# Softmax weights times values: full-width products of head pairs, or one head in each half of PE's columns

## The chip, the cores and the metric

One Trainium2 chip, one of its cores. The metric is the device time of one execution in microseconds. A core has five engines with an instruction queue each: PE (matrix products; its weight loads are listed apart as PEld), DVE and ACT (elementwise work and reductions), POOL, and SP, which here issues most DMAs. Each engine works its queue off in order and waits on semaphores where an operand is not there yet.

## The reference

Block-sparse attention, then a gated feed-forward part (SwiGLU) on the heads put side by side. There are 4 batches, 8 heads, 768 positions, head size 64; blocks are 32 positions, so 24 blocks.

```python
scores = (1 / sqrt(D)) * q @ k.T                      # per batch and head, D = 64
mask = |blk_i - blk_j| <= 1  or  blk_i, blk_j in (0, 23)  or  blk_j in sampled_blocks[blk_i]
attn = softmax(where(mask, scores, -1e9))
x = (attn @ v)                                        # to (4 * 768, 512), heads side by side
g = x @ w_gate                                        # 512 -> 1536
out = (g * sigmoid(g) * (x @ w_val)) @ w_out          # 1536 -> 512
```

A query block from 1 to 22 sees 8 key blocks: its window of three, three sampled ones, and the first and last. Query blocks 0 and 23 see all keys ("full rows").

## The kernel before

**Tiling.** A chunk is half a batch, 384 queries, so there are 8 chunks. A chunk has three query tiles of 128 queries, which are four query blocks each. Per batch, blocks 1 to 12 make the first chunk, and 0, 23 and 13 to 22 the second, whose first tile therefore has two full rows and two sparse blocks. There are 76 sparse blocks in chunks 1 to 7 and 12 in chunk 0.

**Number formats.** Chunk 0 computes in float32 (`first_chunk`, `first_block`, `ffn_first`), while the weights are still being decoded and split. The other chunks use pairs of half-precision numbers: each operand is a high and a low part, and a product is the sum of three (high x high, high x low, low x high). A recorded float32 matmul of the program appears as two in the trace.

**A sparse block** (`block`, L1000). Values of the window are loaded by SP, those of the sampled blocks by an indirect DMA of POOL, into one of three buffers `vring` (the tile `vg`: 256 keys as two times 128 partitions, high and low part, 8 heads of 64). PE makes the scores with 32 queries of four heads in the four 32-column strips of its array (L1041); DVE adds the mask and takes the maximum (L1087), ACT the exponential (L1106), ACT and DVE the high and low weights `pp` (L285, L288). SP transposes them by DMA into `pts` (L1131). Then comes the step that is changed, `product` (L1133): per head pair j, 6 matmuls whose weights are the values of both heads, 128 columns, and whose moving operand is the softmax weights of both heads, 2 x 32 columns. The result has 128 partitions (two heads of 64) and 64 columns, of which the two diagonal quarters are wanted: head 0 with its own 32 columns, head 1 with its own.

**x.** The PSUM tile `pv` is one bank of 512 columns: 4 head pairs x 2 blocks x 64. Two blocks fill it, and then `x_high` copies the wanted quarters to the high part of x (`xt`) on ACT, in two instructions of 64 partitions (L1165), and `x_low` takes the difference on DVE, again two (L1170). The ring of `pv` has two banks. Chunk 0 does the same in float32: `product` at L700 with 8 matmuls, `x_keep` at L716 with two copies. In both, the matmuls of a block are 24 x 128 columns of weights (8 in chunk 0).

**Full rows** (`full_rows`, L795) already put one head in each half of PE's columns, L901 and L902.

**Feed-forward.** For chunks 1 to 7, L1328 is x times w_gate and w_val, 12 matmuls of 384 columns per tile of 128 features, and L1374 is h times w_out, 512 columns. Chunk 0 has L1217 and L1252.

**Order.** Nothing is scheduled at run time. A planner (`Plan`) holds every step as a task with an engine, a time in us, its needs, a rank and the buffers it takes; `plan.order()` runs through them and emits the instructions in the order in which its engines took them. Attention ranks ahead of feed-forward work, so PE's feed-forward matmuls fill in where attention waits. A changed time in the table moves tasks on all engines.

Of the kernel before, what the change touches and what calls it, by code (L numbers as in the profile page):

```python
# [13 lines left out]
ALU = mybir.AluOpType  # L14
AX = mybir.AxisListType

P = 128
B, H, S, D = 4, 8, 768, 64
BLK = 32
# [132 lines left out]
def tile_block_sparse_attn_swiglu(  # L152
# [10 lines left out]
    nc = tc.nc  # L163
# [376 lines left out]
    xts = [Buf("xt") for _ in range(NCH)]  # L540
# [17 lines left out]
    def first_chunk(rank):  # L558
# [16 lines left out]
        for t in range(6):  # L575
# [14 lines left out]
            a = add("PE", 1.6, turn, [k0_loads[t // 2], t_id], rank - 2.0, take=[kp])  # L590
            kept.append(add("DVE" if t % 2 else "ACT", 0.7, keep, [a], rank - 2.0, use=[kp]))

        for sub in range(NSUB):
            qbs = ORDER[0][sub * 4 : sub * 4 + 4]
            regbuf, regs = Buf("pregs"), []
            r0 = rank + 0.3 * sub

            def offsets(qbs=qbs, regs=regs):
                _, r = nc.values_load_multi_w_load_instructions(
                    koff[0:1, qbs[0] : qbs[-1] + 1, :].rearrange("p q j -> p (q j)"),  # L600
                    engines=(mybir.EngineType.Pool,),
                    min_val=0,
                    max_val=S - BLK,
                    skip_runtime_bounds_check_because="sampled_blocks holds block numbers",
                )
                regs.extend(r)

            loaded = add("POOL", 0.8, offsets, [t_tab], r0, take=[regbuf])
            for n, qb in enumerate(qbs):
                if n % 2 == 0:  # L610
                    pv = Buf("pv")
                first_block(qb, sub, n, r0 + 0.05 * n, kT, qs[sub], q_there[sub], kept, regs, regbuf, loaded, pv)

    def first_block(qb, sub, n, rank, kT, q, q_there, kept, regs, regbuf, loaded, pv):
# [4 lines left out]
        vf = vring[slot].rearrange("p c l h d -> p c (l h d)").bitcast(F32)  # L619
        qk, e, dg, pt, pts = Buf("qk"), Buf("e"), Buf("pp"), Buf("ffn"), Buf("pts")  # L620
# [77 lines left out]
            nc.scalar.copy(get(pts, f"pts_0_{qb}").bitcast(F32), pt.tile)  # L698

        def product():  # L700
            if n % 2 == 0:
                get(pv, f"pv_0_{qb}")
            pq = pts.tile.bitcast(F32).rearrange("p (g c u q) -> p g c u q", g=2, c=2, u=4)
            pvv = pv.tile.rearrange("p (j b q) -> p j b q", j=4, b=2)

            for j in range(4):
                g, u = divmod(2 * j, 4)
                for cc in range(2):
                    nc.tensor.matmul(
                        pvv[:, j, n % 2], vf[:, cc, 2 * j * D : (2 * j + 2) * D], pq[:, g, cc, u : u + 2, :],  # L710
                        start=cc == 0, stop=cc == 1,
                    )

        cols = slice(sub * P + (n - 1) * BLK, sub * P + (n + 1) * BLK)

        def x_keep():  # L716
            pvv = pv.tile.rearrange("p (j b q) -> p j b q", j=4, b=2)
            for hh in range(2):
                hs_ = slice(hh * D, (hh + 1) * D)
                nc.scalar.copy(  # L720
                    x_f32()[hs_, :, cols].rearrange("p j (b q) -> p j b q", b=2), pvv[hs_, :, :, hh * BLK : (hh + 1) * BLK]
                )
# [12 lines left out]
        a = in_turn("pv", "PE", 2.4, product, [a, vl, vi], rank, take=[] if n % 2 else [pv], use=[pts] + ([pv] if n % 2 else []))  # L735
# [218 lines left out]
    def attention(ci, rank, qtiles):  # L954
        b, half = divmod(ci, 2)
        bt = batches[b]
        for sub in range(NSUB):
# [35 lines left out]
            pv = None  # L993
            for n, qb in enumerate(sparse):
                r = r0 + 0.05 * n
                if n % 2 == 0:
                    pv = Buf("pv")
                block(ci, b, bt, o, sub, n, qb, qbs.index(qb) * BLK, r, tsc, pv)

    def block(ci, b, bt, o, sub, n, qb, col, rank, tsc, pv):  # L1000
        nq = f"{b}_{qb}"
        slot = sparse_no[0] % RING
        direct = ci == 1
# [127 lines left out]
            nc.sync.dma_start_transpose(get(pts, f"pts_{nq}").rearrange("p (m q) -> p m q", q=P), pp.tile)  # L1131

        def product():  # L1133
            if n % 2 == 0:
                get(pv, f"pv_{nq}")
            pq = pts.tile.rearrange("p (g l c u q) -> p g l c u q", g=2, c=2, l=2, u=4)
            pvv = pv.tile.rearrange("p (j b q) -> p j b q", j=4, b=2)

            for j in range(4):
                g, u = divmod(2 * j, 4)  # L1140
                i = 0
                for cc in range(2):
                    for l, m in ((0, 0), (0, 1), (1, 0)):
                        nc.tensor.matmul(  # L1144
                            pvv[:, j, n % 2],
                            vg[:, cc, l, 2 * j : 2 * j + 2, :],
                            pq[:, g, m, cc, u : u + 2, :],
                            start=i == 0,
                            stop=i == 5,
                        )  # L1150
                        i += 1

        cols = slice(sub * P + col - BLK, sub * P + col + BLK)

        def x_views(hh):
            hs_ = slice(hh * D, (hh + 1) * D)
            pvv = pv.tile.rearrange("p (j b q) -> p j b q", j=4, b=2)
            src = pvv[hs_, :, :, hh * BLK : (hh + 1) * BLK]
            xt = xts[ci].tile
            return [src] + [xt[hs_, l, :, cols].rearrange("p j (b q) -> p j b q", b=2) for l in range(2)]  # L1160

        def x_high():
            for hh in range(2):
                src, hi, _ = x_views(hh)
                nc.scalar.copy(hi, src)  # L1165

        def x_low():
            for hh in range(2):
                src, hi, lo = x_views(hh)
                nc.vector.tensor_tensor(lo, src, hi, op=ALU.subtract)  # L1170
# [21 lines left out]
        if n % 2 == 1:  # L1192
# [267 lines left out]
```

## Time and profile before

| | us |
|---|---|
| median of 3 runs | 867.82 |
| the three runs | 865.56, 867.82, 876.54 |
| the profiled execution, its own time | 876.0 |
| the profiled execution, its span from first to last instruction | 874.2 |
| PE busy in that span | 810.1 |

The profile is of one execution. Its page has the busy time of each engine, the chain of work that ended last (followed back from the last instruction to what released each step), and groups of instructions by line. A group reads: line, engine, operation, out<-in by the program's names, count, then busy us and the mean ns of one, then the idle time before them and what ended it. "128*64" at a matmul is rows times columns of the array that it uses; "128x64" its output, partitions times columns. The duration of a matmul is longer than its distance to the next, since they overlap. A timeline row is start, length, engine, line and count of merged instructions, with the length running to the end of the last.

### The profile page before, as it was taken

To read this page: it belongs to the slowest core of one execution; us is meant where nothing else is said; L and a number is where in the kernel's file an instruction comes from. 1 tells how busy PE (TensorE), PEld (TensorE's weight loads), DVE (VectorE), ACT (ScalarE), POOL (GpSimd) and SP (SyncE) were. 2 spreads that over 40 slices of the span, in tenths; PEclk is the share of its full clock that TensorE was granted. 3 is DMA by queue.
4 is the path that set the end of the run, shared out by engine and by line. 5 is a ranking of instruction groups with operands and counts; after the bars stand their busy time and mean duration, and the time that the engine had idled before them with its cause. 6 is when DMAs were issued, how large, how long until landed. Compare 5 with 4: busy or idle time off the path is not lost.

```text
span 874.2 us, 20573 instructions
## 1 busy us (share of the span) xinstructions
PE 810.1 (93%) x7590; PEld 487.9 (56%) x7590; DVE 602.5 (69%) x1924; ACT 522.0 (60%) x1274; POOL 179.6 (21%) x221
## 2 busy tenths in 40 slices
PE   4788899988799988889999999999999899999998
PEld 3577655544465545556556555665556456655653
DVE  4799799875678876777378857884588578841220
ACT  2666474677765775677358666895466567741220
POOL 3141100002032221132123211241124112310220
PEclk9599899999799997999999999999999999999999
DMA  9989966269974997596978794878767864830001
GB/s 228 297 260 278 261 126 211 55 126 216 183 202 121 185 233 146 110 163 148 265 161 151 161 190 84 182 174 235 172 143 137 164 167 80 164 79 25 1 1 36
DMA packets 189972, 138.13 MB, mean 158 GB/s; under 512 B 138480, under 2 KB 150896, under 8 KB 189872
## 3 DMA queue, kind: packets, MB, share of 16 engines
q1 hardware_dynamic: 184240, 119.52, 60.7%
q0 software_dynamic: 5632, 17.31, 8.3%
q8 instruction: 59, 0.97, 0.5%
q14 instruction: 41, 0.34, 0.1%
HBM read 80.68 MB, written 12.58 MB: 107 GB/s over the span
## 4 chain that ended last, share of the span: by engine, by line
PE 66%; DMA 19%; DVE 10%; issue 2%; SPq 2%; ACT 1%; DVEq 0%; ACTq 0%
PE p L1328 33%; PE po L1374 14%; DMA pts<-pp 8%; PE p L1217 5%; PE pv L1144 5%; PE qk L1041 3%; DMA ptsf<-ppf 2%; DMA w2raw<-in_w_dram 2%; DMA qraw<-in_q_dram 2%; DVE w L314 2%; DVE w L315 2%; DMA qs<-qraw 2%; PE po L1252 1%; DMA w<-in_v_dram 1%; DMA kraw<-in_k_dram 1%
## 5 line engine op out<-in xcount | busy, mean ns | idle before, releaser
L1328 PE MATMUL p<-xt,w 128*128 128x384 f16 x2016 | 344.5, 328 | 1.6 <-ACT xt L1165 0.8
L1328 PEld LDWEIGHTS <-w 128*128 128x128 f16 x2016 | 192.7, 99 | 134.8 <-issue 14.9
L1374 PE MATMUL po<-w,h 128*128 128x512 f16 x756 | 170.8, 379 | 0.0
L1028 POOL DMA_INDIRECT vring<-vd,vidx x76 | 72.2, 950 | 336.8 <-PE pv L1144 264.9
L1349 POOL TENSOR_TENSOR h<-act,h 128x384 f16<-128x384 f32 x84 | 82.1, 979 | 274.5 <-ACT h L1346 274.0
L1374 PEld LDWEIGHTS <-h 128*128 128x128 f16 x756 | 71.5, 98 | 83.5 <-issue 4.2
L1144 PEld LDWEIGHTS <-vring 128*128 128x128 f16 x1824 | 64.8, 100 | 36.3 <-issue 27.8
L1144 PE MATMUL pv<-pts,vring 128*128 128x64 f16 x1824 | 67.8, 195 | 18.4 <-DMA pts<-pp 18.3
L1335 DVE SCALAR_TENSOR_TENSOR act<-act,p 128x384 f32<-128x384 f32 x84 | 46.2, 550 | 55.6 <-ACT act L1332 54.6
L1106 ACT ACTIVATE e<-e,nb,es 128x256 f32<-128x256 f32 x132 | 78.2, 593 | 2.2
L1332 ACT ACTIVATE act<-p,gsc 128x384 f32<-128x384 f32 x84 | 48.6, 578 | 47.9 <-PE p L1328 38.8
L1346 ACT CAST h<-act 128x384 f16<-128x384 f32 x84 | 42.5, 505 | 54.4 <-DVE act L1338 53.7
L288 DVE SCALAR_TENSOR_TENSOR pp<-e,rr,pp 128x256 f16<-128x256 f32 x152 | 71.7, 513 | 4.4 <-ACT pp L285 3.5
L285 ACT ACTIVATE pp<-e,rr 128x256 f16<-128x256 f32 x152 | 68.1, 497 | 7.8 <-issue 2.3
L1217 PE MATMUL p<-xt,w 128*128 128x384 f32 x192 | 66.9, 502 | 3.1 <-ACT xt L720 3.1
L1338 DVE SCALAR_TENSOR_TENSOR act<-act,hs,p 128x384 f32<-128x384 f32 x84 | 51.3, 611 | 21.3 <-PE p L1328 18.9
L1087 DVE CUSTOM_DVE_ANT_1 e<-qk,msk 128x256 f32<-128x256 f32 x132 | 50.2, 418 | 13.5 <-PE qk L1041 7.6
L1217 PEld LDWEIGHTS p<-xt,w 128*128 128x128 f32 x192 | 36.2, 194 | 27.7 <-ACT xt L720 3.3
L1165 ACT CAST xt<-pv 64x256 f16<-64x256 f32 x76 | 27.8, 365 | 36.7 <-PE pv L1144 36.1
L1017 DVE COPY kring<-kst 128x256 f16 x228 | 47.1, 262 | 2.5 <-PE qk L1041 2.2
L1170 DVE TENSOR_TENSOR xt<-pv,xt 64x256 f16<-64x256 f32 x76 | 31.9, 420 | 21.1 <-ACT xt L1165 13.8
L1266 ACT ACTIVATE ot<-po,oc 128x512 f32<-128x512 f32 x21 | 14.4, 686 | 47.0 <-PE po L1374 43.1
(183 smaller groups left out, 1082.9 us busy)
## 6 DMA issues: line engine op xcount, KB each, us to landing
vring<-vd SPq DMA_DIRECT2D x76, 192.0 KB
w1raw<-in_w_dram SPq DMA_DIRECT2D x24, 512.0 KB
qs<-qraw SPq DMA_DIRECT2D x84, 128.0 KB
w2raw<-in_w_dram SPq DMA_DIRECT2D x12, 512.0 KB
vfull<-vd SPq DMA_DIRECT2D x12, 512.0 KB
qraw<-in_q_dram SPq DMA_DIRECT2D x42, 128.0 KB
out_dram<-ot SPq DMA_DIRECT2D x20, 256.0 KB
vraw<-in_v_dram SPq DMA_DIRECT2D x9, 512.0 KB
```

The lines of the kernel that those rows point to most:

```text
L285: nc.scalar.activation(hi, src, AF.Copy, scale=scale)
L288: nc.vector.scalar_tensor_tensor(lo, src, scale, hi, op0=ALU.mult, op1=ALU.subtract)
L1028: nc.gpsimd.indirect_dma_start(vf[0:96, 1, :], None, bt.vd, bass.IndirectOffsetOnAxis(ap=vidx[0:96, qb : qb + 1], axis=0))
L1087: nc.vector.tensor_tensor_reduce(ev[:, g], stv[:, g], o.msk[:, n, :].unsqueeze(2).broadcast_to([P, 8, BLK]), scale=1.0, scalar=-3.0e38, op ...
L1106: nc.scalar.activation(ev[:, g], sv[:, g], AF.Exp, bias=nb_[:, g : g + 1], scale=o.es[:, 0:1], accum_out=c["rs"][:, g : g + 1],)
L1144: nc.tensor.matmul(pvv[:, j, n % 2], vg[:, cc, l, 2 * j : 2 * j + 2, :], pq[:, g, m, cc, u : u + 2, :], start=i == 0, stop=i == 5,)
L1217: nc.tensor.matmul(buf.tile[:, 0:T], wst[m][:, f + 1, k_ * P : (k_ + 1) * P], x_f32()[:, k_, :], start=k_ == 0, stop=k_ == NKT - 1,)
L1328: nc.tensor.matmul(t[:, 0:T], w_[:, f, m, k_, :], xt.tile[:, l, k_, :], start=i == 0, stop=i == 11)
L1332: nc.scalar.activation(get(act, f"act_{ci}_{f}"), pg.tile[:, 0:T], AF.Tanh, scale=c["gsc"][:, f : f + 1])
L1338: nc.vector.scalar_tensor_tensor(act.tile, act.tile, c["hs"][:, 1:2], pw.tile[:, 0:T], op0=ALU.mult, op1=ALU.mult)
L1349: nc.gpsimd.tensor_tensor(hv()[:, 1, :], act.tile, hv()[:, 0, :], op=ALU.subtract)
L1374: nc.tensor.matmul(po.tile, hv[:, l, ts_], wo16[:, f, m, :], start=f == 0 and i == 0, stop=f == NF - 1 and i == 2)
```

## The change

Each matmul of the product is split in two, one per head: 64 columns of weights, 32 moving columns, and the output in its own half of the partitions (0 to 63 or 64 to 127). The two heads' matmuls alternate. A block has 48 matmuls and not 24 (16 and not 8 in chunk 0), of a quarter of the size. All that is computed is wanted, so a block needs 4 x 32 columns of the bank and four blocks fill it. x is taken once per query tile, in one instruction of 128 partitions on ACT and one on DVE; a tile with two full rows has two sparse blocks and takes their half of the bank.

```diff
-                if n % 2 == 0:
+                if n == 0:
                     pv = Buf("pv")
...
         def product():
...
-            pvv = pv.tile.rearrange("p (j b q) -> p j b q", j=4, b=2)
+            pvv = pv.tile.rearrange("p (j b q) -> p j b q", j=4, b=4)
             for j in range(4):
-                g, u = divmod(2 * j, 4)
                 i = 0
                 for cc in range(2):
                     for l, m in ((0, 0), (0, 1), (1, 0)):
-                        nc.tensor.matmul(
-                            pvv[:, j, n % 2],
-                            vg[:, cc, l, 2 * j : 2 * j + 2, :],
-                            pq[:, g, m, cc, u : u + 2, :],
-                            start=i == 0,
-                            stop=i == 5,
-                        )
+                        for hh in range(2):
+                            g, u = divmod(2 * j + hh, 4)
+                            nc.tensor.matmul(
+                                pvv[hh * D : (hh + 1) * D, j, n],
+                                vg[:, cc, l, 2 * j + hh, :],
+                                pq[:, g, m, cc, u, :],
+                                start=i == 0,
+                                stop=i == 5,
+                            )
                         i += 1
-        cols = slice(sub * P + col - BLK, sub * P + col + BLK)
...
+        cols = slice(sub * P + (4 - blocks_) * BLK, (sub + 1) * P)
+        def x_views():
+            src = pv.tile.rearrange("p (j t) -> p j t", j=4)[:, :, 0 : blocks_ * BLK]
+            return [src] + [xts[ci].tile[:, l, :, cols] for l in range(2)]
         def x_high():
-            for hh in range(2):
-                src, hi, _ = x_views(hh)
-                nc.scalar.copy(hi, src)
+            src, hi, _ = x_views()
+            nc.scalar.copy(hi, src)
...
-        a = in_turn("pv", "PE", 0.72, product, [a, vl, vi], rank, take=[pv] if n % 2 == 0 else [], use=[pts] + ([pv] if n % 2 else []))
+        a = in_turn("pv", "PE", 0.5, product, [a, vl, vi], rank, take=[] if n else [pv], use=[pts] + ([pv] if n else []))
         v_read[slot] = [a]
-        if n % 2 == 1:
+        if n == blocks_ - 1:
```

Chunk 0 is changed in the same way (`x_keep` becomes one copy), and its planner time goes from 2.4 to 1.4. The smaller times in the table move other tasks too. Lines below the change have other numbers in the new kernel: L1144 is L1139, L1328 is L1319, L1374 is L1365, L1217 is L1208, L1252 is L1243, L709 is L710, L720 is L716.

The order on PE at a product inside the down projections of a half-precision chunk, from the product's last matmul on. Names: `vring` the values, `pv` and `pts` as above, `nrm_q` the norm of a later query tile, `h` and `po` the down projection. Before:

```order
L1144 LDWEIGHTS vring_113
L1144 MATMUL pv_21_6041<-pts_21_5986,vring_113 128x64
L769 MATMUL nrm_q_6068<-qacc_6019,ones 128x1
L1374 LDWEIGHTS h_2_5041
L1374 MATMUL po_0_6021<-w_102,h_2_5041 128x512
```

At such a place now:

```order
L1139 LDWEIGHTS vring_113
L1139 MATMUL pv_1_4109<-pts_3_4100,vring_113 64x32
L763 MATMUL nrm_q_4387<-qacc_4184,ones 128x1
L1365 LDWEIGHTS h_0_3393
L1365 MATMUL po_2_4395<-w_102,h_0_3393 128x512
```

The product's matmuls now write 64 partitions and their neighbours 128; before, both wrote 128. Along the whole of PE's order, neighbours of different form (128, 64 or 32 columns of the array, or another number of rows) follow each other 252 times before and 369 times now; in chunk 0's attention 24 and 45 times.

The order on PE at the end of chunk 0's attention (`pt`: weights transposed by PE; `nrm_w`: norms of weight tiles; `p`: the first up projection). Before:

```order
L709 MATMUL pv_9_1109<-pts_10_1154,vring_113 128x64 x8
L695 MATMUL pt_12_1179<-dg_12_1167,e_12_1130 128x128 x4
L709 MATMUL pv_11_1197<-pts_11_1170,vring_114 128x64 x8
L360 MATMUL nrm_w_0_1215<-wacc,ones 128x4
L709 MATMUL pv_11_1197<-pts_12_1206,vring_115 128x64 x8
L1217 MATMUL p_0_1249<-xt_123,w_100 128x384 x4
```

Now:

```order
L710 MATMUL pv_9_1143<-pts_10_1160,vring_113 64x32 x16
L763 MATMUL nrm_q_1213<-qacc_516,ones 128x1
L360 MATMUL nrm_w_0_1221<-wacc,ones 128x4
L710 MATMUL pv_9_1143<-pts_11_1211,vring_114 64x32 x16
L695 MATMUL pt_12_1252<-dg_12_1242,e_12_1187 128x128 x4
L710 MATMUL pv_9_1143<-pts_12_1261,vring_115 64x32 x16
L1208 MATMUL p_0_1298<-xt_123,w_100 128x384 x4
```

The last four blocks share one `pv` where two pairs had one each. Further on, chunk 1's first sparse scores stood behind 2 of the 9 groups of four matmuls of chunk 0's down projection (L1252) and stand behind 6 of them now.

The order on ACT at the same place (`wsq`: squares of a decoded weight tile, of w_gate and w_val into `wacc`, of w_out into `oacc`; `xt<-pv`: the copy of x). Before:

```order
L292 ACTIVATE wsq_10_1195,wacc<-w_101 128x512
L698 COPY pts_12_1206<-pt_12_1179 128x512
L292 ACTIVATE wsq_11_1213,wacc<-w_100 128x512
L292 ACTIVATE wsq_11_1226,wacc<-w_101 128x512
L292 ACTIVATE wsq_5_1241,oacc<-w_102 128x512
L720 COPY xt_123<-pv_11_1197 64x4x64 x2
```

Now:

```order
L292 ACTIVATE wsq_8_1219,wacc<-w_100 128x512
L292 ACTIVATE wsq_8_1247,wacc<-w_101 128x512
L698 COPY pts_12_1261<-pt_12_1252 128x512
L292 ACTIVATE wsq_9_1268,wacc<-w_100 128x512
L716 COPY xt_123<-pv_9_1143 128x4x128
```

The last copy of x stood behind 25 squares, one of them of w_out, and stands behind 19 now, all of w_gate and w_val.

More of the change, by code (lines that the diff above doesn't have):

```diff
@@ L734, in first_block @@
         a = in_turn("keep", "ACT", 0.65, keep, [a], rank, take=[pts], use=[pt])
-        a = in_turn("pv", "PE", 2.4, product, [a, vl, vi], rank, take=[] if n % 2 else [pv], use=[pts] + ([pv] if n % 2 else []))
+        a = in_turn("pv", "PE", 1.4, product, [a, vl, vi], rank, take=[] if n else [pv], use=[pts] + ([pv] if n else []))
         v_read[slot] = [a]
-        if n % 2 == 1:
+        if n == 3:
             x_done[0].append(add("ACT", 0.74, x_keep, [a, x_open(0, rank)], rank, use=[pv, xts[0]]))
@@ L995, in attention, with block @@
                 r = r0 + 0.05 * n
-                if n % 2 == 0:
+                if n == 0:
                     pv = Buf("pv")
-                block(ci, b, bt, o, sub, n, qb, qbs.index(qb) * BLK, r, tsc, pv)
-    def block(ci, b, bt, o, sub, n, qb, col, rank, tsc, pv):
+                block(ci, b, bt, o, sub, n, len(sparse), qb, qbs.index(qb) * BLK, r, tsc, pv)
+    def block(ci, b, bt, o, sub, n, blocks_, qb, col, rank, tsc, pv):
         nq = f"{b}_{qb}"
@@ L1133, in product @@
         def product():
[L1134 removed]
+            if n == 0:
                 get(pv, f"pv_{nq}")
             pq = pts.tile.rearrange("p (g l c u q) -> p g l c u q", g=2, c=2, l=2, u=4)
[L1137 removed]
+            pvv = pv.tile.rearrange("p (j b q) -> p j b q", j=4, b=4)
             for j in range(4):
[L1140 removed]
                 i = 0
@@ L1143, in product @@
                     for l, m in ((0, 0), (0, 1), (1, 0)):
[L1144 to L1160 removed]
+                        for hh in range(2):
+                            g, u = divmod(2 * j + hh, 4)
+                            nc.tensor.matmul(
+                                pvv[hh * D : (hh + 1) * D, j, n],
[3 more added lines that the diff above has]
+                                stop=i == 5,
+                            )
+                        i += 1
+        cols = slice(sub * P + (4 - blocks_) * BLK, (sub + 1) * P)
+        def x_views():
+            src = pv.tile.rearrange("p (j t) -> p j t", j=4)[:, :, 0 : blocks_ * BLK]
+            return [src] + [xts[ci].tile[:, l, :, cols] for l in range(2)]
         def x_high():
[L1163 to L1165 removed]
+            src, hi, _ = x_views()
+            nc.scalar.copy(hi, src)
         def x_low():
[L1168 to L1170 removed]
+            src, hi, lo = x_views()
+            nc.vector.tensor_tensor(lo, src, hi, op=ALU.subtract)
         vl = add("SP", 0.18 if new else 0.06, values, bt.v_done + v_read[slot], rank, dma=0.8)
```

14 lines of the change are left out of this document (4 added, 10 removed).

## Prediction, made before the changed kernel ran

> **What bounds the kernel now.** I read the page first: engine shares, then the chain of work that ended last.
>
> ```profile
> span 874.2 us, 20573 instructions
> ## 1 busy us (share of the span) xinstructions
> PE 810.1 (93%) x7590; PEld 487.9 (56%) x7590; DVE 602.5 (69%) x1924; ACT 522.0 (60%) x1274; POOL 179.6 (21%) x221
> ...
> PE 66%; DMA 19%; DVE 10%; issue 2%; SPq 2%; ACT 1%; DVEq 0%; ACTq 0%
> PE p L1328 33%; PE po L1374 14%; DMA pts<-pp 8%; PE p L1217 5%; PE pv L1144 5%; PE qk L1041 3%; DMA ptsf<-ppf 2%; DMA w2raw<-in_w_dram 2%; DMA qraw<-in_q_dram 2%; DVE w L314 2%; DVE w L315 2%; DMA qs<-qraw 2%; PE po L1252 1%; DMA w<-in_v_dram 1%; DMA kraw<-in_k_dram 1%
> ```
>
> PE is the bound, and the product that is changed (L1144) is 5% of the chain, about 44 us. Then the same by stage: chunk 0's attention, its feed-forward part, the other seven chunks, and the last down projections. The columns are length, busy time of PE, PEld, DVE, ACT and POOL, granted clock, DMA share, GB/s.
>
> ```profile
> 0.00:95.00 95.00, 69.17 (x738) 60.19 (x738) 73.19 (x188) 51.65 (x148) 27.76 (x64) 0.84 0.94 266
> 95.00:187.00 92.00, 87.70 (x495) 48.72 (x496) 80.23 (x223) 56.06 (x123) 0.75 (x1) 0.98 0.58 142
> 187.00:786.00 599.00, 569.05 (x5898) 333.97 (x5899) 433.75 (x1483) 397.73 (x975) 140.12 (x145) 0.98 0.77 164
> ```
>
> In the first stage PE is busy 69 of 95 us, while the DMA engines are at 0.94. From 187 to 786 PE is busy 95% of the time: there a microsecond of PE work is nearly a microsecond of span.
>
> **The half-precision product, 76 blocks.** First its pace today: the durations of one matmul (min/median/max), and two products in a table of windows (length, PE busy and count, clock, DMA, GB/s).
>
> ```profile
> L1144 PE MATMUL pv<-pts,vring x1824: 189/193/242, 191.1 to 781.7; 128*128 128x64 f16 x183
> ...
> 201.50:203.00 1.50, 0.86 (x24) 1.00 1.70 98
> ```
>
> 24 matmuls take 0.86 us from the first start to the last end; less one duration, (0.86 - 0.193)/23 = 29 ns from start to start, or 24 x 29 = 0.70 us of PE a block. After the change a block has 48 matmuls, in 24 pairs, one matmul in each half of the columns. A kind row for such a pair stands in the trace already: the full rows' product at L901 and L902 also has 64 columns of weights and puts the two heads in the two halves.
>
> ```profile
> 337.24 1.46 PE L1328 MATMUL p<-xt,w 128*128 128x384 f16 x8
> 338.63 0.25 PE L901 MATMUL pvf<-ptsf,vfull 128*64 128x128 f16 x2
> 338.71 0.20 PE L902 MATMUL pvf<-ptsf,vfull 128*64 128x64 f16 x2
> 338.74 0.23 PE L901 MATMUL pvf<-ptsf,vfull 128*64 128x128 f16 x2
> 338.80 0.20 PE L902 MATMUL pvf<-ptsf,vfull 128*64 128x64 f16 x2
> 338.83 0.23 PE L901 MATMUL pvf<-ptsf,vfull 128*64 128x128 f16 x2
> 338.89 0.20 PE L902 MATMUL pvf<-ptsf,vfull 128*64 128x64 f16 x2
> 339.02 2.12 PE L1328 MATMUL p<-xt,w 128*128 128x384 f16 x12
> ```
>
> Each x2 is a pair, one matmul per half, starting together. A pair of 64 moving columns (L902) is followed after 0.03 us, one of 128 (L901) after 0.06: four matmuls, each with its own weight load, pass in 0.09 us. So the halves really work side by side, and a pair of 64 columns costs what one full-width matmul of 64 costs now. The open question is whether a pair of 32 columns costs less. If the moving columns set the pace, it does; if the weight load does, it does not. Two rows bear on it, of float32 products and of both feed-forward parts:
>
> ```profile
> L709 PE MATMUL pv<-pts,vring x192: 219/275/472, 33.0 to 93.8; 128*128 128x64 f32 x192
> ...
> 74.50:77.00 2.50, 1.90 (x16) 1.90 (x16) 1.00 1.05 271
> ...
> 126.41 20.75 PE p L1217 x64
> ...
> 242.14 11.72 PE p L1328 x72
> ```
>
> Moving columns cost 20.75/64/384 = 0.84 ns each in float32 and 11.72/72/384 = 0.42 ns in half precision. By that, 64 float32 columns need 54 ns, yet L709 goes at (1.90 - 0.275)/15 = 108 ns: 128 columns of weights at 0.84 ns. [...] A 64-column load at 0.42 ns is 27 ns, which also fits L902's 0.03. The bounds for a pair of 32 columns are therefore 32 x 0.42 = 13.6, some 16 ns with the 2 ns that L1144 has over its stream, and 30 ns. I take 28, by the load: 24 x 28 = 0.67 us, 0.024 less than now, x76 = **-1.8 us** (ends: -23.7 and +1.8).
>
> **The change of form.** The same fence shows a cost. The last L1328 before the pair starts at 337.24 + 1.46 - 0.33 = 338.37 and the pair 0.26 later, where L1328 follows itself after 0.163. Behind the last pair, 0.027 of stream, L1328 comes after 0.13. So each way costs 0.10 us more. The product of now pays nothing at that border, since it has the same full-width form as the feed-forward matmuls:
>
> ```profile
> 407.62 0.81 PE L1374 MATMUL po<-w,h 128*128 128x512 f16 x3
> 408.27 0.51 PE L1144 MATMUL pv<-pts,vring 128*128 128x64 f16 x12
> ...
> 291.19 0.62 PE L1041 MATMUL qk<-kring,qs 128*32 128x256 f16 x16
> 291.74 0.87 PE L1144 MATMUL pv<-pts,vring 128*128 128x64 f16 x24
> ```
>
> At 408.27 it starts 0.22 after the last L1374, which is that one's stream of 512 x 0.42 = 0.215. At 291.74, behind the scores in their 32-column form, it starts 0.20 after a stream of 0.107: again about 0.095 more. Counting along PE's two orders, the form changes 228 times outside chunk 0 before and 324 times after: 96 x 0.095 = 9.1 us. PE is idle 5% of the main stage, more where products are dense (the chain below), so I put 0.8 of it on the path: **+7.3 us** (ends: +4 and +9.1).
>
> **The float32 product, 12 blocks.** 32 recorded matmuls in 16 pairs, each load 64 x 0.84 = 54 ns: 16 x 56 = 0.90 us in place of 16 x 108 = 1.73, so -10 us of PE, less 21 more form changes (24 to 45), +2. But this is the stage in which PE is busy 69 of 95 us. What ended it:
>
> ```profile
> 95.78 0.63 ACT L292 ACTIVATE wsq<-w 128x512 bf16<-128x512 f32 x1 [1.87 <-DVE w L315]
> ...
> 96.40 0.73 ACT L720 COPY xt<-pv 64x256 f32<-64x256 f32 x2
> ...
> 97.18 2.39 PE L1217 MATMUL p<-xt,w 128*128 128x384 f32 x4 [3.15 <-ACT xt L720]
> ...
> 97.06 0.43 DVE L313 TENSOR_SCALAR w<-w2raw 128x512 int32<-128x512 int32 x1 [1.38 <-DMA w2raw<-in_w_dram]
> ```
>
> The last copy of x waits on ACT behind the square of a decoded tile of w_out, and DVE decodes as the DMA delivers. In the new ACT order the last copy stands behind 19 such squares and not 25, so chunk 0's feed-forward part may begin up to some 9 us sooner. It has to be handed on through chunk 1, whose end is another matter:
>
> ```profile
> 193.84 7.96 DMA pts<-pp
> ...
> 202.70 1.80 PE po L1252 x4
> ...
> 205.89 8.55 DMA pts<-pp
> ...
> 220.85 8.02 DMA pts<-pp
> ...
> 233.45 1.76 PE p L1328 x5
> ```
>
> The last of chunk 1's products wait for transposes by DMA, 24.5 us in three rows, and chunk 1's feed-forward part waits for them. In the new order chunk 1's first sparse scores come after 6 of the 9 groups of L1252's matmuls and not after 2, so the earlier start is spent on feed-forward work that then no longer fills those waits. I take **-2 us** (ends: -9 and +14, the 14 being four groups of 8 recorded matmuls at 1.80/4 us that stood between the transposes).
>
> **x, once per query tile.** The rows of these copies and of one of full width:
>
> ```profile
> L1165 ACT CAST xt<-pv 64x256 f16<-64x256 f32 x76 | 27.8, 365 | 36.7 <-PE pv L1144 36.1
> L1170 DVE TENSOR_TENSOR xt<-pv,xt 64x256 f16<-64x256 f32 x76 | 31.9, 420 | 21.1 <-ACT xt L1165 13.8
> L698 ACT COPY pts<-pt 128x512 f32<-128x512 f32 x12 | 6.9, 581 | 0.8 <-PE pt L695 0.6
> L1328 PE MATMUL p<-xt,w 128*128 128x384 f16 x2016 | 344.5, 328 | 1.6 <-ACT xt L1165 0.8 <-DVE xt L1170 0.7
> ```
>
> Of 76 copies on each engine 21 remain, 17 of four blocks and 4 of two; at L698's 0.58 us ACT needs 17 x 0.58 + 4 x 0.37 = 11 us and not 28. DVE saves about as much. PE waited for x only 1.6 us in all at L1328, so this is worth **0** (ends: -2, and +2 where a later copy holds up work queued behind it on ACT). PSUM banks are no new wait: two, as before, and each now serves four blocks.
>
> Sum: -1.8 + 7.3 - 2 + 0 = +3.5 us. The profiled execution took 876.0 us (span 874.2), 8 over the median of the three runs, 867.82. Its terms carry over, so I forecast 867.8 + 3.5 = 871 us.
>
> **Rivals.** A: as summed, the load sets the pace. With its ends (-1.8 + 4 - 9 = -7, and +1.8 + 9.1 + 2 + 2 = +15, the 14 being D's) 861 to 883.
> B: the stream sets the pace, 16 ns a pair. Then -23.7 x 0.8 = -19, and -19 + 7.3 - 2 = -14: 854 us. [...] Against it: L709.
> C, on the slow side: the halves' loads follow one another, 27 ns each, so a product takes 48 x 27 = 1.30 us, 76 x 0.60 = +45 on -1.8's place and 7.3 on top: 918 us. It passes 2% once a pair costs over 35 ns ((17.4 - 7.3 + 2)/76/24 = 6.6 ns above 29). Against it: four loads in 0.09 us at L901/L902. [...]
> [...]
> D: the moved order bares the transposes of chunk 1 and nothing gives it back: -1.8 + 7.3 + 14 = +19.5, 887 us.
> That the halves do not run side by side at all is C.
>
> **Chances.** A 0.68, B 0.14, C 0.10, D 0.08. About 2% (17.4 us: below 850.5, above 885.2) is what a measurement of this kernel can tell from no change. Faster by more: a third of B and a little of A, 0.08. Slower: C, half of D and a little of A, 0.16. Within: 0.76. The range 851 to 886 holds A, most of B and half of D.
>
> **What would show it.** The product's row of 48 should last 0.86 us again (24 x 28 ns and one duration of 0.19): 0.57 speaks for B, 1.5 for C. Matmuls of L1328 next to a product should start 0.10 us later than now. Chunk 0's first L1217 should start before 97, and chunk 1's first L1328 near 233. The forecast fails if pairs of 32 columns run below the load time, or if PE's idle time in the main stage moves by more than some 10 us.

## Result: 4.2% slower, and the profile after

| | us |
|---|---|
| median before, all runs together (865.56 to 876.54) | 870.12 |
| median after, 4 runs (901.15 to 916.03) | 910.23 |
| ratio after / before, 95% interval | 1.0421 (1.0303 to 1.0538) |
| the profiled execution after, its own time and span | 916.03, 914.3 |

The ratio leaves out the slowest execution after, 916.03, which is the profiled one (its granted clock of 0.944 lies among the 0.940 to 0.950 of the other three), so it is a little under the quotient of the two medians. It is a loss of 26 to 47 us, where +3.5 was forecast; 910 lies outside the range of 851 to 886.

Parts 1, 4 and 5 of the page after (span, busy time by engine, chain that ended last, and the groups of the down projection and of the product):

```profile
span 914.3 us, 24471 instructions
## 1 busy us (share of the span) xinstructions
PE 831.2 (91%) x9606; PEld 492.2 (54%) x9606; DVE 583.9 (64%) x1869; ACT 503.5 (55%) x1210; POOL 181.1 (20%) x221
...
PE 62%; DMA 17%; DVE 12%; issue 3%; ACT 2%; SPq 2%; DVEq 0%; ACTq 0%
...
L1365 PE MATMUL po<-w,h 128*128 128x512 f16 x756 | 172.9, 382 | 0.4 <-issue 0.4
...
L1139 PE MATMUL pv<-pts,vring 128*64 128x32 f16 x3648 | 78.2, 188 | 24.9 <-DMA pts<-pp 21.8 <-issue 3.2
```

PE is still the bound, with 21 us more busy time; its idle time went from 874.2 - 810.1 = 64 to 83 us. ACT and DVE fell by 18.5 and 18.6 us, from 522.0 and 602.5: that is the saving on the copies of x, and it bought nothing (E5 below). Now where along the span the 40 us arise. Both tables of windows run from one chunk's first up projection (L1319, before L1328; chunk 0: L1208, L1217) to the next chunk's. The columns are stretch, length, busy time of PE, PEld, DVE, ACT and POOL, granted clock, DMA share, GB/s. Before:

```profile
0.00:97.20 97.20, 69.19 (x739) 60.21 (x739) 74.01 (x189) 52.99 (x152) 28.51 (x64) 0.84 0.94 267
97.20:232.60 135.40, 123.41 (x985) 69.28 (x986) 107.64 (x305) 87.61 (x205) 6.87 (x7) 0.97 0.75 160
232.60:336.50 103.90, 96.44 (x927) 56.08 (x926) 79.75 (x284) 71.62 (x169) 26.42 (x27) 0.93 0.82 180
336.50:432.20 95.70, 90.30 (x909) 53.03 (x908) 63.00 (x208) 62.46 (x148) 20.40 (x22) 1.00 0.79 169
432.20:521.70 89.50, 89.38 (x901) 52.11 (x900) 70.86 (x258) 57.55 (x147) 23.20 (x24) 1.00 0.80 165
521.70:612.90 91.20, 91.13 (x927) 53.44 (x926) 64.75 (x216) 65.12 (x154) 21.05 (x22) 1.00 0.73 172
612.90:710.10 97.20, 91.05 (x931) 53.27 (x929) 70.00 (x251) 57.98 (x148) 24.52 (x24) 1.00 0.73 156
710.10:799.90 89.80, 88.95 (x892) 51.77 (x888) 58.51 (x193) 50.78 (x127) 17.66 (x19) 1.00 0.47 100
```

After:

```profile
0.00:86.20 86.20, 58.41 (x931) 48.47 (x931) 64.80 (x174) 46.17 (x132) 29.54 (x64) 0.81 0.94 267
86.20:232.50 146.30, 130.69 (x1224) 76.61 (x1225) 110.35 (x309) 86.96 (x206) 7.26 (x8) 0.90 0.71 162
232.50:351.80 119.30, 101.39 (x1203) 59.27 (x1203) 78.72 (x279) 70.14 (x163) 26.32 (x27) 0.90 0.77 164
351.80:447.30 95.50, 94.98 (x1157) 54.41 (x1157) 61.64 (x201) 58.92 (x139) 21.55 (x23) 0.97 0.68 157
447.30:545.00 97.70, 92.24 (x1189) 52.83 (x1188) 65.74 (x246) 57.01 (x140) 23.14 (x24) 1.00 0.80 164
545.00:648.80 103.80, 96.95 (x1167) 55.27 (x1167) 65.82 (x213) 64.67 (x150) 21.22 (x23) 0.97 0.79 161
648.80:741.80 93.00, 91.38 (x1188) 52.73 (x1187) 68.64 (x244) 53.82 (x135) 23.62 (x24) 1.00 0.74 149
741.80:839.90 98.10, 94.88 (x1159) 53.93 (x1158) 54.18 (x183) 49.93 (x122) 17.49 (x19) 0.98 0.53 96
```

Chunk 0's attention ends 11 us sooner, and the next row gives those 11 back, so chunk 1's feed-forward part begins at 232.5 as before. The loss is in later rows: +15.4 up to chunk 2's, +8.2 and +12.6 up to chunks 4's and 5's, +8.3 up to chunk 7's; the seventh row is 4.2 shorter. In the third row PE is busy 5 us longer, at a lower clock, and idle 10 us longer (17.9, from 7.5). One border shows how. The timeline of PE where chunk 1's down projections run out, before (L1041 scores, L1144 product, L834 scores of full rows):

```profile
285.94 0.62 PE L1041 MATMUL qk<-kring,qs 128*32 128x256 f16 x16
286.50 2.12 PE L1374 MATMUL po<-w,h 128*128 128x512 f16 x9
288.45 0.86 PE L1144 MATMUL pv<-pts,vring 128*128 128x64 f16 x24
...
319.00 2.11 PE L1374 MATMUL po<-w,h 128*128 128x512 f16 x9
321.04 0.84 PE L834 MATMUL qkf<-kst,qs 128*64 128x384 f16 x8
...
336.49 0.75 PE L1328 MATMUL p<-xt,w 128*128 128x384 f16 x3
```

The same border after (L1035 scores, L1139 product, L828 scores of full rows; in brackets an idle time and what ended it):

```profile
290.07 0.62 PE L1035 MATMUL qk<-kring,qs 128*32 128x256 f16 x16
...
303.06 0.62 PE L1035 MATMUL qk<-kring,qs 128*32 128x256 f16 x16
303.62 2.12 PE L1365 MATMUL po<-w,h 128*128 128x512 f16 x9
305.66 0.94 PE L1139 MATMUL pv<-pts,vring 128*64 128x32 f16 x48
...
320.61 4.06 PE L1365 MATMUL po<-w,h 128*128 128x512 f16 x18
324.60 0.94 PE L1139 MATMUL pv<-pts,vring 128*64 128x32 f16 x48
...
331.48 0.94 PE L1139 MATMUL pv<-pts,vring 128*64 128x32 f16 x48 [1.39 <-DMA pts<-pp]
337.25 0.82 PE L828 MATMUL qkf<-kst,qs 128*64 128x384 f16 x2 [4.83 <-DMA qs<-qraw]
...
346.36 1.46 PE L1139 MATMUL pv<-pts,vring 128*64 128x32 f16 x48 [2.60 <-DMA pts<-pp]
...
351.79 0.48 PE L1319 MATMUL p<-xt,w 128*128 128x384 f16 x1 [0.67 <-ACT xt L1157]
```

Before, the first product stands behind one of the scores; after, six scores run ahead, each between two groups of down projections, and the first product comes 15.6 us into the border, where it was 2.5. When the down projections are used up, 8 products are left, where 3 were. They wait for transposes of the weights (`pts`), and the scores of full rows wait for their queries (`qs`, 4.83 us, the longest of these waits), with nothing beside them: 27 us without a feed-forward matmul, where it was 15. Windows of just these stretches, and of the one at the end of chunk 1's attention, after:

```profile
208.80:232.50 23.70, 14.58 (x460) 13.02 (x459) 16.75 (x52) 18.49 (x44) 4.70 (x5) 0.62 0.98 181
324.70:351.80 27.10, 15.40 (x459) 12.49 (x460) 17.95 (x75) 17.25 (x46) 6.86 (x8) 0.74 1.04 213
```

In them PE is busy some 60% of the time, and what it does there it does at a clock of 0.62 and 0.74. So these bare stretches are paid twice: in idle time, and in work at half clock. In the stretches that the clock record of after gives at 0.5, most down projections start 427 ns after one another and up projections 320, where it is 216 and 163 elsewhere; a product's 48 starts span some 1.25 us in place of 0.75. The clock record of the trace divides PE's whole span (PE's busy time in stretches at half clock counts half as lost, which is a little much for the products; for the kernels E1 to E12 see the next section):

| profiled execution | span | PE idle | lost to half clock | the work at full clock |
|---|---|---|---|---|
| before | 874.2 | 64.1 | 20.9 | 789.2 |
| after | 914.3 | 83.1 | 38.2 | 793.0 |
| E1: halves, old order | 880.5 | 57.9 | 29.0 | 793.6 |
| E2: new order, old product | 897.3 | 74.5 | 29.7 | 793.1 |
| E4: halves in chunk 0 alone | 869.3 | 66.9 | 20.9 | 781.5 |
| E8: after, other table | 874.8 | 60.1 | 20.9 | 793.7 |
| E11: values loaded once | 877.4 | 70.0 | 32.9 | 774.6 |
| E12: E11, other table | 877.8 | 76.7 | 24.0 | 777.1 |

Of the 40 us only 4 seem to be more work, with 19 of idle time and 17 of half clock. But chunk 0's float32 product needs 8 us less (789.2 to 781.5 in E4), and E4's time shows no gain from that. So the same division follows for the part from chunk 1's first up projection to chunk 7's, rows 3 to 8 of the tables of windows:

| profiled execution, rows 3 to 8 | length | PE idle | lost to half clock | the work at full clock |
|---|---|---|---|---|
| before | 567.3 | 20.1 | 5.7 | 541.6 |
| after | 607.4 | 35.6 | 16.1 | 555.7 |
| E1: halves, old order | 575.8 | 15.1 | 7.1 | 553.6 |
| E2: new order, old product | 588.7 | 32.7 | 11.1 | 544.9 |
| E3: after, 0.95 in the table | 587.6 | 24.5 | 8.1 | 555.0 |
| E5: after, old table | 577.1 | 17.5 | 5.4 | 554.3 |
| E6: old product, chunk 0's entry | 583.8 | 28.7 | 10.2 | 544.9 |
| E8: after, other table | 569.9 | 11.6 | 4.4 | 553.9 |
| E9: 113 more form changes | 574.6 | 16.2 | 5.5 | 553.0 |

Here all of the 40 us appear: 14 are work, 15.5 idle time and 10.4 half clock. The work goes with the product (542 to 545 with the old one, 554 to 556 with the new one; the 3 us between kernels with the same product are the uncertainty of this count), and idle time and half clock go with the order.

### The profile page after: what moved, and what is told of

It reads as the page before. It is cut to its first block, busy times and chain, and to the rows that moved or that the text cites. A ratio compares the mean times of both kernels' runs of the same rounds, so it can differ in the third digit from the quotient of the medians.

```text
span 914.3 us, 24471 instructions
## 1 busy us (share of the span) xinstructions
PE 831.2 (91%) x9606; PEld 492.2 (54%) x9606; DVE 583.9 (64%) x1869; ACT 503.5 (55%) x1210; POOL 181.1 (20%) x221
## 4 chain that ended last, share of the span: by engine, by line
PE 62%; DMA 17%; DVE 12%; issue 3%; ACT 2%; SPq 2%; DVEq 0%; ACTq 0%
PE p L1319 31%; PE po L1365 15%; DMA pts<-pp 7%; PE pv L1139 6%; PE qk L1035 3%; PE po L1243 3%; DMA w1raw<-in_w_dram 2%; DMA qs<-qraw 2%; DMA kraw<-in_k_dram 2%; DVE w L314 2%; DVE w L315 2%; DMA qraw<-in_q_dram 1%; PE qkf L828 1%; DMA w<-in_v_dram 1%; DVE w L313 1%
## 5 line engine op out<-in xcount | busy, mean ns | idle before, releaser
L1319 PE MATMUL p<-xt,w 128*128 128x384 f16 x2016 | 351.0, 331 | 3.4 <-ACT xt L1157 1.7
L1319 PEld LDWEIGHTS <-w 128*128 128x128 f16 x2016 | 193.7, 99 | 141.4 <-issue 23.3
L1365 PE MATMUL po<-w,h 128*128 128x512 f16 x756 | 172.9, 382 | 0.4 <-issue 0.4
L1365 PEld LDWEIGHTS <-h 128*128 128x128 f16 x756 | 71.6, 99 | 86.1 <-issue 7.2
L1139 PE MATMUL pv<-pts,vring 128*64 128x32 f16 x3648 | 78.2, 188 | 24.9 <-DMA pts<-pp 21.8
L1139 PEld LDWEIGHTS <-vring 128*64 128x64 f16 x3648 | 72.3, 119 | 47.6 <-issue 45.8
L288 DVE SCALAR_TENSOR_TENSOR pp<-e,rr,pp 128x256 f16<-128x256 f32 x152 | 74.5, 530 | 5.5 <-ACT pp L285 5.5
L1208 PE MATMUL p<-xt,w 128*128 128x384 f32 x192 | 66.1, 505 | 0.7 <-ACT xt L716 0.7
L1208 PEld LDWEIGHTS p<-xt,w 128*128 128x128 f32 x192 | 37.4, 197 | 26.0 <-issue 2.4
L1035 PE MATMUL qk<-kring,qs 128*32 128x256 f16 x1056 | 41.2, 277 | 0.8 <-ACT ef L850 0.6
L292 ACT ACTIVATE wsq<-w 128x512 bf16<-128x512 f32 x36 | 22.6, 629 | 34.1 <-DVE w L315 29.5
```

The source lines that it names most:

```text
L288: nc.vector.scalar_tensor_tensor(lo, src, scale, hi, op0=ALU.mult, op1=ALU.subtract)
L1035: nc.tensor.matmul(stv[u * BLK : (u + 1) * BLK, g].rearrange("p s k -> p (s k)"), o.q[:, l, h // 2, h % 2, col : col + BLK], kg[:, h].rear ...
L1139: nc.tensor.matmul(pvv[hh * D : (hh + 1) * D, j, n], vg[:, cc, l, 2 * j + hh, :], pq[:, g, m, cc, u, :], start=i == 0, stop=i == 5,)
L1208: nc.tensor.matmul(buf.tile[:, 0:T], wst[m][:, f + 1, k_ * P : (k_ + 1) * P], x_f32()[:, k_, :], start=k_ == 0, stop=k_ == NKT - 1,)
L1319: nc.tensor.matmul(t[:, 0:T], w_[:, f, m, k_, :], xt.tile[:, l, k_, :], start=i == 0, stop=i == 11)
L1365: nc.tensor.matmul(po.tile, hv[:, l, ts_], wo16[:, f, m, :], start=f == 0 and i == 0, stop=f == NF - 1 and i == 2)
```

## Experiments

The kernels ran in three groups, E1 to E4, E5 to E8 and E9 to E12; a group shares one chip and its runs of the kernel before. In the expectations O is the theory that the moved order costs most, F that each form change is paid in full, L that the weight load sets the pace of a pair; T divides the order's cost between the two entries of the table. "Halves" is a product with one head in each half.

| | product | table: half precision, chunk 0 | median (range) | ratio to before, 95% |
|---|---|---|---|---|
| E1 | halves, x as before | 0.72, 2.4 | 884.64 (882.18–888.22) | 1.0195 (1.0113–1.0276) |
| E2 | as before | 0.5, 1.4 | 894.63 (893.44–899.07) | 1.0292 (1.0215–1.0368) |
| E3 | as after | 0.95, 1.4 | 894.74 (893.91–895.12) | 1.0294 (1.0218–1.0370) |
| E4 | halves in chunk 0 alone | 0.72, 2.4 | 870.07 (866.05–877.69) | 1.0013 (0.9970–1.0056) |
| E5 | as after | 0.72, 2.4 | 887.16 (884.48–889.07) | 1.0192 (1.0158–1.0225) |
| E6 | as before | 0.72, 1.4 | 889.87 (882.20–891.19) | 1.0196 (1.0135–1.0258) |
| E7 | as before | 0.5, 2.4 | 889.38 (885.73–890.88) | 1.0196 (1.0157–1.0235) |
| E8 | as after | 0.95, 2.4 | 877.82 (876.64–878.52) | 1.0066 (1.0026–1.0106) |
| E9 | as before, 113 more form changes | 0.72, 2.4 | 880.30 (878.11–883.10) | 1.0135 (1.0056–1.0213) |
| E10 | E1 with 64 moving columns | 0.72, 2.4 | 887.23 (883.70–889.93) | 1.0214 (1.0136–1.0292) |
| E11 | v_hi loaded once for both weights | 0.72, 2.4 | 883.17 (879.13–891.89) | 1.0190 (1.0089–1.0291) |
| E12 | as E11 | 0.95, 2.4 | 881.88 (875.22–886.70) | 1.0143 (1.0046–1.0240) |

**E1 and E2: the product or the order.** E1 puts the halves into the kernel before and changes nothing else: the two results go to the wanted quarters of the old layout, so tasks, table, copies and the order on all engines stay (and the same in chunk 0).

```diff
-                        nc.tensor.matmul(
-                            pvv[:, j, n % 2],
-                            vg[:, cc, l, 2 * j : 2 * j + 2, :],
...
+                        for hh in range(2):
+                            g, u = divmod(2 * j + hh, 4)
+                            nc.tensor.matmul(
+                                pvv[hh * D : (hh + 1) * D, j, n % 2, hh * BLK : (hh + 1) * BLK],
+                                vg[:, cc, l, 2 * j + hh, :],
```

> The kernel before with both products in halves, 48 and 16 matmuls of 64 columns, each written to the quarter of the bank that is read today; the planner's table, the tasks, the copies of x and so every engine's order stay as before. The new product's own rows give 32 ns a pair (0.78 us a block against 0.70) and some 96 form changes of 0.1 us: +6 and +9 us. Theory O (the order that the planner made of the smaller times costs the rest, some 24 us): 870 + 15 = 885 us. Theory W (the product's own work and what waits for it make the whole difference, the order none of it): about 905 to 910 us.

E2 is the reverse: the product of before, and only the two numbers of the table.

```diff
-        a = in_turn("pv", "PE", 2.4, product, [a, vl, vi], rank, take=[] if n % 2 else [pv], use=[pts] + ([pv] if n % 2 else []))
+        a = in_turn("pv", "PE", 1.4, product, [a, vl, vi], rank, take=[] if n % 2 else [pv], use=[pts] + ([pv] if n % 2 else []))
...
-        a = in_turn("pv", "PE", 0.72, product, [a, vl, vi], rank, take=[pv] if n % 2 == 0 else [], use=[pts] + ([pv] if n % 2 else []))
+        a = in_turn("pv", "PE", 0.5, product, [a, vl, vi], rank, take=[pv] if n % 2 == 0 else [], use=[pts] + ([pv] if n % 2 else []))
```

> The kernel before with only the two times in the planner's table changed, 0.72 to 0.5 and 2.4 to 1.4; products and copies as before. O: the order alone costs, 885 to 895 us. W: within 5 us of the kernel before, 865 to 875 us.

E1 takes 15.5 us more than before, E2 25.5. Together 41, the whole loss of 40. The order alone, with not one matmul changed, is the greater part. The second table of the division agrees: E1 has 12 us more work than before and no more idle time, E2 has 18 more of idle time and half clock. Its bare stretch stands at the same border as after's (windows of E2):

```profile
327.40:349.00 21.60, 10.65 (x189) 8.05 (x187) 12.50 (x53) 10.96 (x32) 5.53 (x6) 0.76 1.11 210
```

**E3: a true time for the product in the table.** In the kernel after, 0.5 becomes 0.95, which is about the product (0.79) and one and a half changes of form.

```diff
-        a = in_turn("pv", "PE", 0.5, product, [a, vl, vi], rank, take=[] if n else [pv], use=[pts] + ([pv] if n else []))
+        a = in_turn("pv", "PE", 0.95, product, [a, vl, vi], rank, take=[] if n else [pv], use=[pts] + ([pv] if n else []))
```

> The changed kernel with 0.95 in place of 0.5 in the table for the half-precision product (its 0.78 us and a form change and a half). O: the order fits the work again, 885 to 890 us. W: as the changed kernel, 900 to 910 us.

894.7, between what O and W expected: some 15 us come back, the rest of the order's cost does not.

**E4: chunk 0's product alone.** E1's edit in the float32 product, nothing else.

> The kernel before with only chunk 0's float32 product in halves, in the old order. PE saves 0.8 us in each of 12 products in a stage that the decoding of weights and the DMA bound. O and W alike: within 4 us of the kernel before, 866 to 872 us. A theory by which chunk 0's product is on the path: 860 us.

0.1%, with an interval of 0.4% (some 4 us) to either side: of the 8 us that PE works less in chunk 0 no gain is seen. The first row of the windows before goes with it: in that stretch PE is busy 69 of 97 us, with the DMA engines at 0.94.

**E5 to E8: which entry of the table.** E5 is the kernel after with the old table, E6 and E7 the kernel before with one new entry each, E8 the kernel after with 0.95 and chunk 0's old 2.4. E8's edit:

```diff
-        a = in_turn("pv", "PE", 1.4, product, [a, vl, vi], rank, take=[] if n else [pv], use=[pts] + ([pv] if n else []))
+        a = in_turn("pv", "PE", 2.4, product, [a, vl, vi], rank, take=[] if n else [pv], use=[pts] + ([pv] if n else []))
...
-        a = in_turn("pv", "PE", 0.5, product, [a, vl, vi], rank, take=[] if n else [pv], use=[pts] + ([pv] if n else []))
+        a = in_turn("pv", "PE", 0.95, product, [a, vl, vi], rank, take=[] if n else [pv], use=[pts] + ([pv] if n else []))
```

> The changed kernel (halves, x once per query tile) with the table of before, 0.72 and 2.4. Of the 41 us, the halves in the old order cost 15 and the table on the old kernel 25; with a true half-precision time in the table 10 us over the halves in the old order are left. Theory T (those 10 come from chunk 0's 1.4): 884 to 888 us here. Theory X (from taking x once per query tile): 894 us or more here.

> The kernel before with only chunk 0's time changed in the table, 2.4 to 1.4. T: some 10 of the 25 us that the two entries cost together, 880 us. Rival (all of it from the half-precision entry): 870 us.

> The kernel before with only the half-precision time changed in the table, 0.72 to 0.5. T: some 15 of the 25 us, 885 us. Rival: all 25 us, 895 us.

> The changed kernel with 0.95 and 2.4 in the table. T: 884 to 888 us, the halves' own cost alone. X: 894 us, as with 0.95 and 1.4.

E5 loses what E1 loses (17 and 15.5 us): taking x once per query tile, in the order that goes with the old table, neither costs nor gains. E6 and E7 each lose 19, and both entries together (E2) 25: the costs don't add up, and T's division falls. That E1 and E2 add up to the whole loss is therefore no rule. E8 is the best with the new product, 0.7% over before and below both values expected. Its stretch at the border of chunks 1 and 2:

```profile
319.20:330.10 10.90, 7.65 (x171) 5.67 (x170) 7.21 (x29) 7.01 (x17) 2.76 (x3) 0.70 0.99 220
```

10.9 us and not 27. The four kernels with the code of after, E3, E5, E8 and after itself, differ in two numbers of the table alone and span 877.8 to 910.2. In the trace's starts, the stretches of over 5 us between two feed-forward matmuls add up to 71 us in after, 53 in E2 and in E3, 43 in E7, 30 in before and 11 in E8. But 25 in E6 and 14 in E5, which are slow too. By the second table of the division, E5's loss is the work of the halves; E6, with the old product, has 13 us more of idle time and half clock, spread over several of these rows.

E8 does the same work as E1 and E5, but has 16 us of idle time and half clock where before has 26. So E1's 15.5 us are the price of the halves in one order, and not a fixed one. Nor does a truer entry make a better order: chunk 0's new product takes 0.95 us, so 1.4 is nearer to it than 2.4, yet E3 with 1.4 is 17 us slower than E8 with 2.4. Why the planner's order is better in one case than in another stays open, and so does whether E8's table would make the kernel with the old product faster: it was not tried.

**E9: form changes by themselves.** The kernel before, with the last of a block's 24 matmuls made as two of 64 columns of weights, each with all 64 moving columns; so each product ends in another form and 113 changes are added.

```diff
+                        for hs_ in [slice(0, P)] if j < 3 or i < 5 else [slice(0, D), slice(D, P)]:
                             nc.tensor.matmul(
-                                pvv[:, j, n % 2],
...
+                                pvv[hs_, j, n % 2],
+                                vg[:, cc, l, 2 * j : 2 * j + 2, :].rearrange("p h d -> p (h d)")[:, hs_],
...
```

> The kernel before, tasks and order untouched; of the 24 full-width matmuls of a product the last alone is made as two of 64 columns of weights (each with both heads' 64 moving columns). That adds 113 changes of form in chunks 1 to 7, at 0.097 us each 11 us of PE, and next to no other work. Theory F (PE pays each change of form on the path; the halves' 15 us in the old order are about 9 of form and 6 of pace): 878 to 881 us. Rival (changes of form are hidden, the pace and the number of instructions cost the 15): 870 to 872 us.

+10.6 us, or 94 ns for each of 113 (interval 4.9 to 18.5 us, 43 to 164 ns each). The work at full clock of rows 3 to 8 rises by 11.4 us. Full payment fits, but the interval doesn't tell it from 0.8 of it.

**E10: does the stream count.** E1, but each half streams the 64 columns of both heads, twice as many.

```diff
-                                pvv[hh * D : (hh + 1) * D, j, n % 2, hh * BLK : (hh + 1) * BLK],
+                                pvv[hh * D : (hh + 1) * D, j, n % 2],
...
-                                pq[:, g, m, cc, u, :],
+                                pq[:, g, m, cc, u : u + 2, :],
```

> The halves in the old order, but each half's matmul streams both heads' 64 moving columns in place of its own 32, with the same 48 weight loads of 64 columns a product; the unwanted quarters are written and not read. Theory L (the weight load sets the pace): pairs stay at 32 ns and the time at that of the halves in the old order, 883 to 887 us. Rival (the moving columns or the output set part of it): pairs of 40 to 45 ns, 895 to 908 us.

2.6 us above E1, with intervals that overlap. The timeline of PE in E10 at one product (L1147 there, L1377 the down projection):

```profile
297.77 1.46 PE L1377 MATMUL po<-w,h 128*128 128x512 f16 x6
299.16 0.95 PE L1147 MATMUL pv<-pts,vring 128*64 128x64 f16 x48
300.04 0.62 PE L1043 MATMUL qk<-kring,qs 128*32 128x256 f16 x16
```

0.95 us with 64 moving columns, 0.94 with 32 (the rows of after above). So the moving columns do not set the pace. Whether the weight load does, or some other step that each matmul of a half needs, is not shown: every matmul in halves has a load of 64 columns of its own, and no run changes that.

**E11 and E12: fewer loads.** If loads set the pace, v_hi, the high part of the values, need not be loaded twice: the high and low weights stream side by side behind one load, 32 matmuls a block and not 48. Their two sums are added by an instruction on DVE for every two blocks, ahead of the copies of x.

```diff
-                    for l, m in ((0, 0), (0, 1), (1, 0)):
+                    for l in range(2):
...
-                                pq[:, g, m, cc, u, :],
+                                pq[:, g, 0, cc, u, :] if l else pq[:, g, :, cc, u, :],
...
+            a = add("DVE", 0.7, x_sum, [a], rank, take=[xs], use=[pv])
```

> From L a cheaper product follows: the high values are loaded once for both the high and the low weights (64 moving columns, side by side in the bank), so 32 matmuls a block and not 48, 16 loads a half and not 24; DVE adds the two sums, once for two blocks, before x is taken. Table 0.72 and 2.4. Product 16 x 32 ns = 0.51 us, 0.26 less than the halves and 0.19 less than full width, x76 = -19 us against the changed kernel with the table 0.95 and 2.4 (878): 859 to 866 us if PE is the bound throughout. Rival (the added sums on DVE and the order give it back): 870 us or more.

> The same with 0.95 in the table, to see how much the planner's order alone moves it: PE work as in the run with 0.72, so 859 to 866 us by work alone; by the order up to 10 us either way.

Both miss, at 883 and 882. The product itself is shorter (timeline of PE in E11):

```profile
299.04 0.68 PE L1139 MATMUL pv<-pts,vring 128*64 128x64 f16 x32
299.65 0.62 PE L1035 MATMUL qk<-kring,qs 128*32 128x256 f16 x16
```

0.68 where after has 0.94 (its 16 pairs still take (0.68 - 0.19)/15 = 33 ns), and over the whole span the work at full clock falls by 14.6 and 12.1 us against before, 8 of them in chunk 0, where E4 gained nothing. But idle time and half clock rise by 17.9 in E11 and 15.7 in E12, which takes all of it back. E11 has a bare stretch of 27 us at the border of chunks 1 and 2 (windows):

```profile
318.70:345.40 26.70, 13.06 (x299) 9.45 (x298) 18.04 (x70) 15.77 (x43) 7.17 (x7) 0.62 1.04 189
```

E12 has 14 there and is no faster, so that is not the whole of it. Whether the added sum on DVE or again the order brings the idle time was not tried apart. No version was found that beats the kernel before.

## Why the prediction was wrong

**The failed step: the term of -2 us (ends: -9 and +14) in the part on the float32 product, as the whole price of the moved order.** The prediction followed the order to the end of chunk 1's attention and stopped there. That far it was right: "the earlier start is spent" (chunk 0's first L1208 at 86.2, 11 us sooner), and chunk 1's first up projection stands at 232.5, as it said ("near 233"). But the two numbers move tasks in all eight chunks, and every later border was put at nothing, unlooked at. E2 measured the order by itself: +25.5 us, nearly twice the upper end of 14. What the order brought there is idle time and half clock of PE: 52 us in rows 3 to 8 of after, 26 in before.

**Rival D had the mechanism at one place only.** "The moved order bares the transposes of chunk 1" did come about (23.7 us without a feed-forward matmul from 208.8 on), and again at the border to chunk 2. D priced four groups of down projections at their length, 14 us; the price has a second part that it lacked, the half clock in a bare stretch.

**The half-precision product: -1.8, measured near +7; this term was mis-sized.** The stream does not set the pace (so B is out), as E10 shows: 0.95 us with 64 moving columns, 0.94 with 32. But a pair takes 33 ns and not 28: (0.94 - 0.183)/23 in the rows of after, by 0.183 for its last matmul, against 29 before. 76 blocks x 24 pairs x 4 ns = +7. The 28 had been taken as the load alone, 27 ns, at the 0.42 ns of a moving column: the author's estimate, and no run shows a load of 27 ns, or that the load sets the pace. The prediction's own row of 29 ns speaks against that rate: there each matmul loads 128 columns, which would be 54 ns. And L902's 0.03 stood between streams of 0.06: two pairs at 33 ns fit into the 0.09 of both, so that row did not test the load. The starts in the trace show 3 to 4 ns between the two of a pair and 28 to 29 to the next pair. C's serial loads, 1.30 us a product, did not occur: with the distance to the next pair a product takes 0.76 + 0.03 = 0.79 us.

**The form changes: right.** 0.09 to 0.10 us each way, counted 117 more in all (96 of them outside chunk 0). The rows of after:

```profile
426.07 2.12 PE L1365 MATMUL po<-w,h 128*128 128x512 f16 x9
428.12 0.94 PE L1139 MATMUL pv<-pts,vring 128*64 128x32 f16 x48
428.98 3.19 PE L1365 MATMUL po<-w,h 128*128 128x512 f16 x14
```

With the mean durations of the groups, the last L1365 before the product starts at 426.07 + 2.12 - 0.38 = 427.81, and the product 0.31 later, of which 0.215 is stream. Its own last matmul starts at 428.12 + 0.94 - 0.18 = 428.88, and L1365 0.10 later by these rounded rows, 0.115 by the starts in the trace, of which 0.013 is stream. The share of 0.8 on the path is a little low by E9's size, within its interval.

**The float32 product's pace: right, and worth nothing.** 16 pairs pass in 0.95 us (0.90 forecast); in E4 none of it is seen at the end.

**x, once per query tile: 0, as forecast.** E5 against E1 (17 and 15.5 us), though their orders are not quite the same.

So with the measured sizes, halves in an unmoved order come to 7 + 96 x 0.097 = +16, chunk 0 left out, where E1 has 15.5 (9.8 to 24 by its interval), and the order adds 25. The limit set for failure, "PE's idle time in the main stage moves by more than some 10 us", is what happened: 35.6 us in rows 3 to 8, from 20.1. The profile of before gave a hint of it: a main stage that is 95% busy, with feed-forward work beside most waits, has much to lose by another order.

## What to carry to other kernels

In a kernel whose order is planned from a table of durations, a changed number is a change of its own on all engines: try it alone on the old code, and the new code in the old order, before judging either. Look at each border where the filler work runs out, not at the first one only, and count what runs there at half clock (38 us of PE time over the whole of after) as well as what waits. Splitting these small matmuls over parts of the array saved nothing, since a pair takes its 33 ns with half the stream too, and it costs a change of form, 0.09 to 0.10 us, wherever a neighbour has the full width.

## What the runs showed of the hardware

- A pair of matmuls side by side, each with its own load of 64 columns, takes 33 ns, whether 32 or 64 columns stream behind it (0.94 and 0.95 us for 48 matmuls).
- A change of form costs 93 to 102 ns beyond the stream in the starts of the kernel after, whichever two of the forms of 128, 64 and 32 columns meet (for example 0.309 us from a down projection to a product, where the next down projection follows after 0.216).
- In the kernel after, half clock comes in stretches of 3.4, 6.8, 10.2, 13.7 and 23.9 us, after some 7 us in which PE was busy 35 to 80%: it had not stood still. What brings it on is not shown. By the clock record half clock cost 38 us of PE time in the kernel after, and 21 in the one before.
